# Attention's scores, maxima, p @ v and output projection ordered by an account of the PSUM buffers

## The chip, the cores and the metric

The kernel runs on one core of one Trainium2 chip. The metric is the device time of one execution in microseconds. The kernel before took 1170.13 us (median of three runs, 1167.9 to 1170.29). One more execution was recorded by the hardware profiler; the rows below are from it.

Engines are named as in the profile: PE is TensorE's matrix multiplication and PEld its weight load, DVE is VectorE, ACT is ScalarE, POOL is GpSimd, SP is the queue that issues the DMAs.

## The reference

One transformer block in which attention and a dense layer run side by side on the same normalised input, S = 2048 rows, D = 448, 16 heads of width 28 that share one key and one value head:

```python
x = A_x
xn = _layernorm(x, axis=-1)
q = (xn @ wq).reshape(B, S, H, Dh).transpose(0, 2, 1, 3)
k, v = xn @ wk, xn @ wv
scores = jnp.einsum("bhqd,bkd->bhqk", q, k) * (Dh ** -0.5)
p = softmax(scores, axis=-1)
o = jnp.einsum("bhqk,bkd->bhqd", p, v)
attn = o.transpose(0, 2, 1, 3).reshape(B, S, H * Dh) @ wo
mlp = relu(xn @ w1) @ w2
return x + attn + mlp
```

## The kernel before, in words

The program has three stretches. First the input is normalised and multiplied by the three projections; q, k and v go to DRAM in two parts each (a rounded value and its remainder), from where they are loaded again as stacks that contract over 112 rows. Then comes the dense layer, 28 tasks of two steps (`mlp_up`, `mlp_down`). Last comes attention. The change touches only attention, which starts when the last task of the dense layer has been issued.

**Units and blocks.** Attention has 16 units (`NU`): four blocks of 512 queries by four groups of four heads. A unit has 16 key blocks (`NKB`) of 128 keys. For one key block of one unit PE makes four scores (L557, one per head, 128 keys by 512 queries, in a PSUM tile `a`, after the maxima are done also in `m`), ACT takes the exponential of each (L559, into an SBUF tile `p`), and `pv` (L425) multiplies the four `p` by the values: 4 calls of L429 that add into 32 of the 128 partitions each of the PSUM tile `o`. The profile shows each call as two matmuls, so 8 per block.

**Maxima.** The softmax subtracts each query's maximum over the keys. It is found ahead of the scores: a second product (L306, queries by 512 keys, PSUM tile `m`) that DVE reduces (L310). A unit needs 64 of these products, all units 1024. 192 of them run during the dense layer's last tasks, 832 in attention; when a unit has all of its maxima, `max_all` (L318 to L320) joins them on DVE and `max_rows` (L323) turns them on PE, copies them on ACT (L329) and writes them by DMA into the two extra rows of the unit's query stack, which is why a unit's scores can start only after that.

**Buffers.** PSUM has 3 tiles `a`, 4 tiles `m` and 1 tile `o`. An `m` comes free when DVE has read it, an `a` when ACT has; a matmul into a tile that has not come free waits on PE, and all of PE's later work behind it, since PE takes its instructions in order. There are 24 tiles `p`, enough for six blocks.

**The order.** The order is written out per key block, called a step. `FIRST_OF` = "SMSMSMSMVX" and `OTHERS` = "MSMSMSMSX" say what PE gets: S is a score with its exponential, M a maximum, V the `pv` of the four blocks of the group before (`PVB` = 4), X the side work due at this step. `n_max` leaves out some M so that the 832 are spread evenly over the blocks up to eight before the last unit. So each V has four blocks, and comes once every four blocks, behind the first four scores of the next group.

**What follows a unit.** When a unit's last block has been through `pv`, ACT copies `o` out (L434), `dens` sends the sums of the exponentials to a tile `d` by four small DMAs (L457), and side work is put down: `recips` four steps on (DVE's reciprocal L463, then a DMA to DRAM and four back into `rb`), `normalized` seven steps on (POOL, L472 to L476), and after the last unit of a query block four `o_proj` (L479, 12 matmuls each into an `m`, added to `acc` by DVE at L491 and written out), one per step from nine steps on. For the last query block the first three groups of heads are projected by `o_proj_part` (L496) in 12 pieces of three matmuls, and `finish` (L509) does the last unit. `load_stack(u + 4)` (L287) issues the four DMAs of a later unit's query stack at the start of unit `u`.

## Time and profile before

| | us |
|---|---|
| runs: median (lowest to highest) | 1170.13 (1167.9 to 1170.29) |
| the profiled execution | 1169.32 |
| its span, first to last instruction | 1167.5 |
| granted clock of PE, mean | 0.999 |
| start of attention (first L557) in the span | 395.9 |
| last maximum's product ends, about | 1093.8 |
| last `pv` starts | 1154.6 |

The profiled execution's time is 1.8 us longer than its span. A row of a timeline is: start and length in us, engine, line, operation, tiles written and read, shapes, how many instructions were joined in the row, and in square brackets the idle time of the engine just before it with what ended it. A row of the waits is: engine, tile and line, what it waited for, total us, times, longest us. A row of the windows is: stretch, its length, then for each engine its busy us and the number of its instructions. In a busy group: line, engine, operation, tiles, shapes, count, busy us, mean ns of one, idle us before them.

### The profile page before, as it was taken

To read this page: it belongs to the slowest core of one execution; us is meant where nothing else is said; L and a number is where in the kernel's file an instruction comes from. 1 tells how busy PE (TensorE), PEld (TensorE's weight loads), DVE (VectorE), ACT (ScalarE), POOL (GpSimd) and SP (SyncE) were. 2 spreads that over 40 slices of the span, in tenths; PEclk is the share of its full clock that TensorE was granted. 3 is DMA by queue.
4 is the path that set the end of the run, shared out by engine and by line. 5 is a ranking of instruction groups with operands and counts; after the bars stand their busy time and mean duration, and the time that the engine had idled before them with its cause. 6 is when DMAs were issued, how large, how long until landed. Compare 5 with 4: busy or idle time off the path is not lost.

```text
span 1167.5 us, 15326 instructions
## 1 busy us (share of the span) xinstructions
PE 1151.4 (99%) x5908; PEld 731.5 (63%) x5908; DVE 791.2 (68%) x1393; ACT 583.6 (50%) x1166; POOL 115.5 (10%) x96
## 2 busy tenths in 40 slices
PE   8999999999999999999999999999999999999998
PEld 7888888778888754545456555556555545655435
DVE  6733338887788777777776878786687778586402
ACT  4311110001100467667665767675576767476784
POOL 2323022020200201010010101101011011010110
PEclk9999999999999999999999999999999999999999
DMA  8581610001000101101102010111101100000000
GB/s 254 207 177 43 145 34 1 1 1 35 1 1 1 29 1 42 32 11 43 28 16 64 11 42 16 28 33 34 43 8 42 33 11 11 32 12 1 11 10 32
DMA packets 34431, 45.94 MB, mean 39 GB/s; under 512 B 10056, under 2 KB 21000, under 8 KB 34192
## 3 DMA queue, kind: packets, MB, share of 16 engines
q1 hardware_dynamic: 34360, 44.98, 14.5%
q8 instruction: 46, 0.75, 0.3%
q14 instruction: 25, 0.20, 0.1%
HBM read 32.37 MB, written 12.18 MB: 38 GB/s over the span
## 4 chain that ended last, share of the span: by engine, by line
PE 83%; DVE 12%; ACT 3%; issue 1%; SPq 0%; DMA 0%; POOL 0%; ACTq 0%; DVEq 0%
PE a L557 21%; PE o L429 19%; PE m L306 18%; PE a L161 12%; DVE nmx L310 8%; PE a L164 3%; PE m L486 3%; PE a L360 3%; PE o L360 3%; DVE acc L365 2%; ACT p L559 2%; DVE hL L348 1%; ACT hH L347 1%; PE m L504 1%; PE m L557 1%
## 5 line engine op out<-in xcount | busy, mean ns | idle before, releaser
L310 DVE TENSOR_REDUCE nmx<-m 128x1 f32<-128x512 f32 x1024 | 625.9, 680 | 147.6 <-PE m L306 147.3
L559 ACT ACTIVATE p<-a 128x512 f32<-128x512 f32 x975 | 494.2, 658 | 181.1 <-PE a L557 180.5
L306 PE MATMUL m<-kst,qst 112*128 112x512 f32 x1024 | 401.8, 408 | 3.4 <-DVE nmx L310 1.8
L557 PE MATMUL a<-qst,kst 114*128 114x512 f32 x975 | 397.1, 419 | 5.0 <-ACT p L559 4.6
L557 PEld LDWEIGHTS a<-qst,kst 114*128 114x128 f32 x975 | 183.3, 188 | 141.1 <-ACT p L559 122.5
L306 PEld LDWEIGHTS m<-kst,qst 112*128 112x128 f32 x1024 | 194.2, 190 | 83.9 <-issue 42.8
L429 PE MATMUL o<-p,vtile 128*32 128x512 f32 x2048 | 233.0, 595 | 0.0
L347 ACT ACTIVATE hH<-a 128x512 fp32r<-128x512 f32 x56 | 33.5, 599 | 274.1 <-PE a L164 274.1
L429 PEld LDWEIGHTS o<-p,vtile 128*32 128x32 f32 x2048 | 60.0, 109 | 138.1 <-issue 132.6
L161 PE MATMUL a<-xH,w 128*128 128x512 f32 x432 | 135.1, 394 | 1.9 <-POOL w L126 1.9
L348 DVE SCALAR_TENSOR_TENSOR hL<-a,hH 128x512 fp32r<-128x512 f32 x56 | 38.7, 692 | 91.3 <-ACT hH L347 91.2
L161 PEld LDWEIGHTS a<-xH,w 128*128 128x128 f32 x432 | 81.4, 189 | 18.5 <-POOL w L126 2.2
L472 POOL TENSOR_TENSOR on<-rb,oS 128x512 f32<-128x512 f32 x15 | 19.4, 1293 | 671.2 <-DMA rb<-rscr 298.9
L161 PE MATMUL a<-xL,w 128*128 128x512 f32 x216 | 84.9, 393 | 0.0
L360 PE MATMUL a<-w,hH 128*128 128x448 f32 x224 | 63.8, 366 | 0.0
L360 PE MATMUL o<-w,hH 128*128 128x448 f32 x224 | 63.7, 366 | 0.0
L161 PEld LDWEIGHTS a<-xL,w 128*128 128x128 f32 x216 | 40.8, 189 | 8.9 <-DVE xL L212 0.3
L360 PEld LDWEIGHTS a<-w,hH 128*128 128x128 f32 x224 | 42.0, 188 | 5.8
L360 PEld LDWEIGHTS o<-w,hH 128*128 128x128 f32 x224 | 42.2, 188 | 4.6
L164 PE MATMUL a<-xR,w 128*128 128x512 f32 x144 | 44.9, 393 | 0.1
L365 DVE TENSOR_TENSOR acc<-o,acc 128x448 f32<-128x448 f32 x56 | 34.6, 618 | 14.1 <-PE o L360 14.1
L360 PE MATMUL o<-w,hL 128*128 128x448 f32 x112 | 40.9, 365 | 0.0
(94 smaller groups left out, 572.3 us busy)
## 6 DMA issues: line engine op xcount, KB each, us to landing
qst<-qscr SPq DMA_DIRECT2D x64, 224.0 KB
qscr<-qs SPq DMA_DIRECT2D x16, 512.0 KB
rb<-rscr SPq DMA_DIRECT2D x60, 64.0 KB
acc<-in_A_x SPq DMA_DIRECT2D x16, 224.0 KB
out<-acc SPq DMA_DIRECT2D x16, 224.0 KB
stg<-in_B_w SPq DMA_DIRECT2D x7, 448.0 KB
stg<-in_B_w SPq DMA_DIRECT2D x7, 384.0 KB
d<-oS SPq DMA_DIRECT2D x60, 2.0 KB
```

The lines of the kernel that those rows point to most:

```text
L161: nc.tensor.matmul(ps, lhs[:, wi, c, cols], xm[:, c, xs], start=n == 0, stop=False)
L164: nc.tensor.matmul(ps, lhs[:, wi, DC, cols], xR[:, xs], start=False, stop=wi == 1)
L306: nc.tensor.matmul(pm, qst[u][0:KQ, j, s * P : (s + 1) * P], kst[0:KQ, k0 : k0 + QB], start=True, stop=True)
L310: nc.vector.tensor_reduce(nmx[u][:, n, h : h + 1], pm, axis=AX.X, op=ALU.max)
L347: nc.scalar.activation(hH[:, f], ph, AF.Relu)
L348: nc.vector.scalar_tensor_tensor(hL[:, f], ph, 0.0, hH[:, f].bitcast(F32), op0=ALU.max, op1=ALU.subtract)
L360: nc.tensor.matmul(py[:, 0:D], hm[:, f, i * P : (i + 1) * P], wd[:, wi, f, :], start=n == 0, stop=n == 3 * FC - 1)
L365: nc.vector.tensor_tensor(acc[:, t, :], py[:, 0:D], acc[:, t, :], op=ALU.add)
L429: nc.tensor.matmul(o_acc[u][32 * j : 32 * j + 32], vtile[:, kb, :], p, start=kb == 0, stop=kb == NKB - 1)
L486: nc.tensor.matmul(py[:, 0:D], om[:, i * P : (i + 1) * P], wm[:, g, :], start=n == 0, stop=n == 3 * NHG - 1)
L557: nc.tensor.matmul(pt, kst[0 : KQ + 2, kb * P : (kb + 1) * P], st, start=True, stop=True)
L559: nc.scalar.activation(p, pt, AF.Exp, scale=SCALE)
```

## The change

The order per step is replaced by a loop that keeps an account in nanoseconds: `t` is PE's time, `act` and `dve` the starts of the two readers' latest work, `rings` the times at which the buffers `a` and `m` come free, `blocks` the key blocks whose scores are issued, with the time at which their exponentials are done. The account runs when the program is built; the program on the chip is again a fixed order. In each round of the loop one thing is issued:

- a score or a maximum while a buffer for it is free by the account (of the two, the one whose reader has less to do; maxima keep to the same even spread, up to `SLACK` = 6 ahead or behind);
- else, if an `o_proj` is waiting in `fill` and an `m` is free within 100 ns, and fewer than `MIN_V` = 3 blocks are ready or no maxima are left, that `o_proj`;
- else `pv` of all blocks of this unit that are ready, if they are three or more (two, if no buffer comes free within 100 ns); a unit's last blocks are taken together;
- else it waits for whichever buffer comes first.

So the number of blocks per V is no longer fixed. The side work of a unit is counted from the block being scored when its last `pv` is issued: `recips` 3, `normalized` 6 and the projections 8 blocks later, where before it was 4, 7 and 9 from the next unit's start. `o_proj` goes to `fill` and is issued by the rule above; `o_proj_part` is now 4 pieces of nine matmuls. `load_stack(u + 4)` is issued after the first block of unit `u` instead of ahead of it. Buffers, tiles, arithmetic and the number of instructions of each kind stay as they were. After the last maximum a score takes an `m` when that ring's next buffer is free earlier than that of `a` by the account and nothing is in `fill`, where before it alternated.

```diff
-    ppool = ctx.enter_context(tc.tile_pool(name="ppool", bufs=(PVB + 2) * HG, reuse_waits="tile"))
+    P_BUFS = 24
+    ppool = ctx.enter_context(tc.tile_pool(name="ppool", bufs=P_BUFS, reuse_waits="tile"))
...
-    FIRST_OF, OTHERS = "SMSMSMSMVX", "MSMSMSMSX"
-    side = {}
+    side, fill = {}, []
...
-            step = (u + 1) * NKB
             dens(u)
-            at(step + 4, recips, u)
-            at(step + 7, normalized, u)
+            at(step + 3, recips, u)
+            at(step + 6, normalized, u)
             if units[u][1] == NHG - 1:
-                for i in range(TPB):
-                    at(step + 9 + i, o_proj, u, i)
+                at(step + 8, fill.extend, [(o_proj, (u, i)) for i in range(TPB)])
             if u == NU - 2:
...
+                at(step + 8, fill.extend, [(o_proj_part, (u, i)) for i in range(TPB)])
...
+    T_MM, T_PV, T_MODE, T_EXP, T_MAX, T_PROJ = 232, 860, 280, 478, 597, 202
+    TO_ACT, TO_DVE, ACT_OUT, DVE_OUT = 430, 450, 745, 730
+    left, SLACK, MIN_V, WAIT = len(mx_todo), 6, 3, 100
+    spread_over = HG * ((NU - 1) * NKB - 8)
...
+    def ready():
+        n = 0
+        while n < len(blocks) and blocks[n][3] <= t and blocks[n][0] == blocks[0][0]:
+            n += 1
+        return n if n and (blocks[0][1] or t >= acc_free) else 0
...
+    while n_s < n_all or blocks:
+        step = n_s // HG
+        room = n_s < n_all and n_open < P_BUFS
+        n_max = left - len(mx_todo)
+        due = min(left, n_s * left // spread_over)
+        wants = mx_todo and n_max < due + SLACK and mx_todo[0][0] in qst
+        rest = rings["M"][0] - t
+        pool = "M" if not mx_todo and not fill and rings["M"][0] < rings["A"][0] else "A"
+        wait_s = max(0, rings[pool][0] - t) if room and (n_max + SLACK >= due or not wants) else None
+        wait_m = max(0, rest) if wants else None
+        n_v = ready()
+        tail = NKB - blocks[0][1] if blocks else 0
+        if n_v < tail <= MIN_V + 1 and room:
+            n_v = 0
+        least = min((w for w in (wait_s, wait_m) if w is not None), default=None)
+        if least == 0:
+            if wait_s == 0 and wait_m == 0:
+                what = "S" if act <= dve else "M"
+            else:
+                what = "S" if wait_s == 0 else "M"
+        elif fill and rest <= WAIT and (not mx_todo or n_v < MIN_V):
+            what = "F"
+        elif n_v >= MIN_V or n_v >= 2 and (least is None or least > WAIT) or n_v and (n_s == n_all or not room):
+            what = "V"
...
+        if what == "S":
+            t = max(t, rings[pool][0])
...
+            u, kb, p = score(pool)
...
+            act = max(act + T_EXP, t + TO_ACT)
+            rings[pool] = rings[pool][1:] + [act + ACT_OUT]
+            t += T_MM
...
+                if kb == 0 and u:
+                    load_stack(u + 4)
...
+        elif what == "V":
+            for u, kb, pp, _ in blocks[:n_v]:
+                pv(step, u, kb, pp)
+                t += T_PV
...
```

**Where the order moves.** PE in the middle of attention, before: the end of a group of four blocks and the `pv` of the group ahead of it. `a` is a score's tile, `m` a maximum's, `o` the accumulator of `pv`, `qst` and `kst` the query and key stacks.

```order
L557 MATMUL a<-qst,kst 128x512 x3
L306 MATMUL m<-kst,qst 128x512
L557 MATMUL a<-qst,kst 128x512
L306 MATMUL m<-kst,qst 128x512
L557 MATMUL a<-qst,kst 128x512
L306 MATMUL m<-kst,qst 128x512
L557 MATMUL a<-qst,kst 128x512
L306 MATMUL m<-kst,qst 128x512
L429 MATMUL o<-p,vtile 32x512 x16
L306 MATMUL m<-kst,qst 128x512
```

The same engine and stage after the change, where 11 scores and 10 maxima alternate between two `pv`.

```order
L544 MATMUL a<-qst,kst 128x512
L307 MATMUL m<-kst,qst 128x512
L544 MATMUL a<-qst,kst 128x512
L427 MATMUL o<-p,vtile 32x512 x12
L307 MATMUL m<-kst,qst 128x512
L544 MATMUL a<-qst,kst 128x512
```

A `pv` of four blocks (16 calls) after 29 to 31 scores and maxima has become one of two, three or four blocks, mostly after about 21, and the places where scores stood without a maximum between them are nearly gone. Over all of attention 64 batches of four blocks have become 92: 33 of two blocks, 47 of three, 11 of four and one of five. 81 of them come before the last maximum is far behind and hold 229 blocks; the last 11 hold 27.

PE near the end, where no maxima are left, before:

```order
L557 MATMUL a<-qst,kst 128x512
L557 MATMUL m<-qst,kst 128x512
L429 MATMUL o<-p,vtile 32x512 x16
L557 MATMUL a<-qst,kst 128x512
L557 MATMUL m<-qst,kst 128x512
```

And after the change:

```order
L544 MATMUL a<-qst,kst 128x512
L427 MATMUL o<-p,vtile 32x512 x8
L544 MATMUL m<-qst,kst 128x512 x2
L544 MATMUL a<-qst,kst 128x512
L544 MATMUL m<-qst,kst 128x512
```

Before, 16 scores stand between two `pv` of four blocks here; now 8 stand between two of two blocks.

More of the change, by code (lines that the diff above doesn't have):

```diff
@@ L492, in o_proj, with o_proj_part @@
         nc.sync.dma_start(out[t * P : (t + 1) * P, :], acc[:, t, :])
-    o_parts = {}
-    def o_proj_part(u, i, g):
+    def o_proj_part(u, i):
         b, last_g = units[u]
-        if g == 0:
-            o_parts[i] = psM.tile([P, QB], F32, name="m")
-        oH, oL = o_hl[b * NHG + g]
-        py, c = o_parts[i][:, 0:D], slice(i * P, (i + 1) * P)
-        for n, (om, wm) in enumerate(((oH, woH), (oH, woL), (oL, woH))):
-            nc.tensor.matmul(py, om[:, c], wm[:, g, :], start=g == 0 and n == 0, stop=g == last_g and n == 2)
-        if g == last_g:
-            t = b * TPB + i
-            nc.vector.tensor_tensor(acc[:, t, :], py, acc[:, t, :], op=ALU.add)
+        pt = psM.tile([P, QB], F32, name="m")
+        py, c = pt[:, 0:D], slice(i * P, (i + 1) * P)
+        for g in range(last_g + 1):
+            oH, oL = o_hl[b * NHG + g]
+            for n, (om, wm) in enumerate(((oH, woH), (oH, woL), (oL, woH))):
+                nc.tensor.matmul(py, om[:, c], wm[:, g, :], start=g == 0 and n == 0, stop=g == last_g and n == 2)
+        t = b * TPB + i
+        nc.vector.tensor_tensor(acc[:, t, :], py, acc[:, t, :], op=ALU.add)
     def finish(u):
@@ L535, in finish @@
             nc.sync.dma_start(out[t * P : (t + 1) * P, :], acc[:, t, :])
-    left = len(mx_todo)
-    spread_over = (NU - 1) * NKB - 8
-    group, ready = [], []
-    for u in range(NU):
-        if u:
-            load_stack(u + 4)
-        for kb in range(NKB):
-            step = u * NKB + kb
-            n_max = max(0, min(left, (step + 1) * left // spread_over) - (left - len(mx_todo)))
-            order = FIRST_OF if kb % PVB == 0 else OTHERS
-            skip = order.count("M") - n_max if kb % PVB == 0 else 0
-            ps = []
-            for what in order:
-                if what == "S":
-                    if mx_todo or len(ps) % 2 == 0:
-                        pt = psA.tile([P, QB], F32, name="a")
-                    else:
-                        pt = psM.tile([P, QB], F32, name="m")
-                    st = qst[u][0 : KQ + 2, len(ps), :]
-                    nc.tensor.matmul(pt, kst[0 : KQ + 2, kb * P : (kb + 1) * P], st, start=True, stop=True)
-                    p = ppool.tile([P, QB], F32, name="p")
-                    nc.scalar.activation(p, pt, AF.Exp, scale=SCALE)
-                    ps.append(p)
-                elif what == "M":
-                    if skip > 0 or not n_max:
-                        skip -= 1
-                        continue
-                    n_max -= 1
-                    done = max_tile()
-                    if done is not None:
-                        at(step + 1, max_rows, done, max_all(done))
-                elif what == "X":
-                    for f, a in side.pop(step, ()):
-                        f(*a)
-                elif what == "V":
-                    for done in ready:
-                        pv(*done)
-                    ready = []
-            group.append((u, kb, ps))
-            if len(group) == PVB:
-                ready, group = group, []
@@ L579, in attention_plus_mlp, with score @@
-    assert not side and not mx_todo
-    for done in ready:
-        pv(*done)
+    T_MM, T_PV, T_MODE, T_EXP, T_MAX, T_PROJ = 232, 860, 280, 478, 597, 202
+    TO_ACT, TO_DVE, ACT_OUT, DVE_OUT = 430, 450, 745, 730
+    left, SLACK, MIN_V, WAIT = len(mx_todo), 6, 3, 100
+    spread_over = HG * ((NU - 1) * NKB - 8)
+    t = act = dve = acc_free = 0
+    rings = {"A": [0] * NA, "M": [0] * NM}
+    blocks, ps, n_s, n_open = [], [], 0, 0
+    def score(pool):
+        u, kb, j = n_s // (HG * NKB), n_s // HG % NKB, n_s % HG
+        pt = psA.tile([P, QB], F32, name="a") if pool == "A" else psM.tile([P, QB], F32, name="m")
+        st = qst[u][0 : KQ + 2, j, :]
+        nc.tensor.matmul(pt, kst[0 : KQ + 2, kb * P : (kb + 1) * P], st, start=True, stop=True)
+        p = ppool.tile([P, QB], F32, name="p")
+        nc.scalar.activation(p, pt, AF.Exp, scale=SCALE)
+        return u, kb, p
@@ L585 @@
+    assert not side and not mx_todo and not fill, (side.keys(), len(mx_todo), fill)
 _INS = ["A_x", "A_wq", "A_wk", "A_wv", "A_wo", "B_w1", "B_w2"]
```

51 lines of the change are left out of this document (44 added, 7 removed).

## The prediction

> **What bounds the kernel now.** I read the page's busy times first, then the windows of attention's stages, the waits in the longest, and its timeline.
>
> ```profile
> PE 1151.4 (99%) x5908; PEld 731.5 (63%) x5908; DVE 791.2 (68%) x1393; ACT 583.6 (50%) x1166; POOL 115.5 (10%) x96
> PEclk9999999999999999999999999999999999999999
> ```
>
> ```profile
> 406.80:1095.50 688.70, 687.12 (x3708) 367.95 (x3707) 511.73 (x880) 464.42 (x938) 47.80 (x43) 1.00 0.10 25
> 1095.50:1154.60 59.10, 55.65 (x322) 27.91 (x321) 3.32 (x8) 46.96 (x96) 3.20 (x3) 1.00 0.02 6
> ```
>
> ```profile
> ACT p L559 <- PE a L557: 172.2, 54, 6.3
> DVE nmx L310 <- PE m L306: 146.3, 54, 3.1
> PEld a L557 <- ACT p L559: 108.7, 508, 0.5
> ```
>
> The clock is granted in full all along, so distances between PE's rows can be compared anywhere. The stage with maxima takes 688.7 us. PE's busy time there is 687.1, but a matmul's row is longer than the distance to the next one, so that figure says nothing of gaps. ACT is busy 67% of the stage and DVE 74%. They wait in turn: 54 times (about once per group of four blocks) ACT and DVE stand idle until PE brings new work, and 508 times a weight load for a score waits for ACT. Engines that wait for each other by turns mean that no engine is full. The Trainium skill (Perfetto Trace Analysis, Identifying the Most-Contended Engine) says that matmul busy time does not tell how near PE is to its limit; by that rule PE's 99% is no bar to a gain, and the timeline agrees:
>
> ```profile
> 694.00 3.64 PE L429 MATMUL o<-p,vtile 128*32 128x512 f32 x32
> 697.57 0.50 PE L306 MATMUL m<-kst,qst 112*128 112x512 f32 x1
> 697.91 0.39 PE L557 MATMUL a<-qst,kst 114*128 114x512 f32 x1
> 698.11 8.54 DVE L310 TENSOR_REDUCE nmx<-m 128x1 f32<-128x512 f32 x14 [2.31 <-PE m L306]
> 698.34 7.95 ACT L559 ACTIVATE p<-a 128x512 f32<-128x512 f32 x16 [3.58 <-PE a L557]
> 698.38 0.40 PE L557 MATMUL a<-qst,kst 114*128 114x512 f32 x1
> ...
> 698.85 0.64 PE L557 MATMUL a<-qst,kst 114*128 114x512 f32 x2
> 698.99 0.19 PEld L557 LDWEIGHTS a<-qst,kst 114*128 114x128 f32 x1 [0.18 <-ACT p L559]
> ...
> 700.06 0.41 PE L557 MATMUL a<-qst,kst 114*128 114x512 f32 x1
> 700.54 0.42 PE L557 MATMUL a<-qst,kst 114*128 114x512 f32 x1
> ...
> 702.50 1.40 PE L557 MATMUL a<-qst,kst 114*128 114x512 f32 x3
> 703.74 0.40 PE L306 MATMUL m<-kst,qst 112*128 112x512 f32 x1
> ...
> 705.21 0.39 PE L306 MATMUL m<-kst,qst 112*128 112x512 f32 x1
> 705.53 3.64 PE L429 MATMUL o<-p,vtile 128*32 128x512 f32 x32
> ...
> 709.10 0.50 PE L306 MATMUL m<-kst,qst 112*128 112x512 f32 x1
> ```
>
> One group lasts from 705.53 back to 694.00, 11.53 us. Unhindered, a score or maximum follows the last by 0.233 (697.91 to 698.38 holds two). A `pv` of four blocks holds PE for 3.57 (705.53 to 709.10); ACT and DVE run dry in it, 3.58 and 2.31 us. Afterwards PE is too fast for them: a pair of score and maximum takes 0.49 (702.50 is five pairs after 700.06), ACT's pace, and where three scores stand alone (702.50 to 703.74) each takes 0.41. The order puts `pv` where PE would have work anyway and lets PE wait where `pv` could have run.
>
> **PE's own work in attention.** Further rows, of the page, the chain and the timeline: groups of the two readers, an `o_proj`, one of the pieces of `o_proj_part`, attention's start and end.
>
> ```profile
> L310 DVE TENSOR_REDUCE nmx<-m 128x1 f32<-128x512 f32 x1024 | 625.9, 680 | 147.6 <-PE m L306 147.3
> ```
>
> ```profile
> 609.43 2.44 PE m L486 x12
> ```
>
> ```profile
> 395.88 0.63 PE L557 MATMUL a<-qst,kst 114*128 114x512 f32 x2
> 398.28 0.50 PE L557 MATMUL a<-qst,kst 114*128 114x512 f32 x1 [1.07 <-ACT p L559]
> ```
>
> ```profile
> 1137.84 0.37 PE L504 MATMUL m<-woH,oH 128*128 128x448 f32 x1
> 1138.05 0.37 PE L504 MATMUL m<-woL,oH 128*128 128x448 f32 x1
> ...
> 1154.62 3.64 PE L429 MATMUL o<-p,vtile 128*32 128x512 f32 x32
> ```
>
> From 395.9 to the end of the last `pv` (1154.62 + 3.57 = 1158.2) are 762.3 us. The work in it:
> - 1024 scores and 832 maxima by 0.233: 432.4.
> - 256 blocks of `pv`. The 32 matmuls of four blocks stand in eight fours, 0.43 apart, so 0.86 a block and 3.44 of the 3.57: 220.2.
> - What a batch costs beside its blocks: on entry 705.53 - 705.21 - 0.233 = 0.09, on leaving 3.57 - 3.44 = 0.13, and the first matmul behind it 697.91 - 697.57 - 0.233 = 0.11. Together 0.33; 64 batches, 21.1.
> - 12 `o_proj` by 2.45 (the row, 2.44): 29.4. The 36 matmuls of `o_proj_part` by 0.205: 7.4.
>
> Sum 710.5. So PE waits 51.8 us of the 762.3. Of these, 42 lie in the stage with maxima: its 57 groups have 912 scores and 815 maxima (402.4), 57 batches (57 x 3.77 = 214.9) and 29.4 of projection, 646.7 of 688.7.
>
> **The change, part by part.**
>
> *More batches.* 92 instead of 64: 28 x 0.33 = 9.2 us more on PE. The Trainium skill (TensorEngine Tiling, Key Properties) says that a change of tiling mode drains TensorE, and `pv` runs in 32-column tiles between full-width matmuls, which speaks against shorter batches. A drain to the modelled end of the last matmul would put the entry at 0.16 (its 0.39 less 0.233) in place of 0.09: 28 x 0.07 = 2 us more. The rows start `pv` before that end, so I keep 9.2.
>
> *Waits between two `pv`.* Now mostly 11 scores and 10 maxima in turn. Do they fit without a wait? A reader starts 0.43 after its matmul (697.91 to 698.34). DVE takes one per (8.54 - 0.68) / 13 = 0.605, ACT one per 0.488 (702.50 is five pairs after 700.06). A buffer is back 0.76 after its reader's start (698.34 to the fourth score: the load at 698.99, its matmul 0.11 later, as elsewhere). With four `m`, the tenth maximum needs the sixth read: 0.43 + 5 x 0.605 + 0.76 = 4.22, and PE comes to it at 9 x 0.466 = 4.19: 0.03 short. With three `a`, the eleventh score needs the eighth's reader: 0.43 + 7 x 0.488 + 0.76 = 4.61, and PE comes at 4.66: no wait. Then `pv` follows, 1.72 + 0.33 or 2.58 + 0.33, in which both readers finish what is left (three tiles, 1.8 us for DVE). So a segment of 21 costs about 0.04 of waiting; over 81 batches 3 us in place of 42. Bounds: nothing, and 0.25 a segment (one load's wait of 0.18 and some), 20 us.
>
> *`pv` and its exponentials.* In the 81 batches the last `p` read belongs to a score at least three scores back. The score issued last could only start once the exponential three before it was done, since there are three `a`. So `pv` waits for nothing new; nothing is queued behind such a wait.
>
> *The end, without maxima.* Rows of before:
>
> ```profile
> 1104.86 3.64 PE L429 MATMUL o<-p,vtile 128*32 128x512 f32 x32
> ...
> 1111.44 0.64 ACT L559 ACTIVATE p<-m 128x512 f32<-128x512 f32 x1
> ...
> 1111.92 0.65 ACT L559 ACTIVATE p<-a 128x512 f32<-128x512 f32 x1
> ...
> 1112.62 0.50 PE L557 MATMUL a<-qst,kst 114*128 114x512 f32 x1 [0.24 <-ACT p L559]
> ...
> 1114.27 3.64 PE L429 MATMUL o<-p,vtile 128*32 128x512 f32 x32
> ```
>
> Four blocks take 9.41. ACT's pace here is 0.48. Now eight scores and two blocks alternate: PE 8 x 0.233 + 1.72 + 0.33 = 3.9, ACT 8 x 0.48 = 3.8, and seven buffers keep ACT supplied during the 2.05 of a batch. PE is the bound by a little, 7.8 for four blocks. The gain is in the 51.8. At the very end the last `pv` (three blocks, straight behind eight scores) needs the eighth exponential: 0.54 + 7 x 0.48 + 0.76 = 4.7 after the batch before, while PE reaches that block at 0.24 + 1.86 + 1.72 = 3.8: 0.9 us of waiting that was not there before.
>
> *Start.* The 1.1 us at 398.28 (ACT's first exponentials come late) stay.
>
> *Side work.* `recips` now comes at least 13 scores after the unit's last `pv`. DVE would wait if `d` had not landed, and the maxima behind it, and so PE. Rows of a unit's end in the last stage:
>
> ```profile
> 1118.10 0.60 ACT L434 ACTIVATE oS<-o 128x512 f32<-128x512 f32 x1 [1.12 <-issue]
> 1118.72 2.44 SPq L457 DMA_DIRECT2D d<-oS  x4
> 1122.35 0.25 DVE L463 RECIPROCAL r<-d 128x16 f32<-128x16 f32 x1 [26.20 <-DMA d<-oS]
> ```
>
> `d` lands 3.6 us after its issue, which comes right behind the copy of `o`, some 0.9 us after the `pv`. Thirteen scores are a segment (4.9), a batch (2.05) and two pairs (0.9): 7.8 us. So 6.9 us lie between issue and use; 3.3 to spare, cost nothing. On SP's queue the stack load (four DMAs) now stands right before `d` in four units, with two small DMAs between in a fifth, behind `d` in six; the stack itself is wanted by maxima only a unit later. `o_proj` fills PE as before; its DVE addition waits as before. Both at nothing.
>
> *Sum.* 762.3 becomes 710.5 + 9.2 + 3.2 + 0.9 + 1.1 = 724.9, 37.4 less. The profiled execution took 1169.3 (span 1167.5 and 1.8 around it), 0.8 below the runs' median. So 1169.3 - 37.4 = 1131.9, and against the median's level 1132.7: **1133 us**.
>
> **The rivals.**
>
> *The readers still set the pace.* If ACT and DVE hold PE to 0.49 a pair, as in the rows at 700, the 830 pairs lose 0.024 each, 20 us: 1133 - 3 + 20 = **1150**. For it: the account uses 0.478, 0.597, 0.28 and 0.745 where I read 0.488, 0.605, 0.33 and 0.76, all a little short, so it may think buffers free that aren't. Against: pairs run at 0.47 when the rings are empty (697.91 to 698.85), and a segment now ends before they are full.
>
> *`d` comes late.* In five units `d` queues behind a stack load.
>
> ```profile
> qst<-qscr SPq DMA_DIRECT2D x64, 224.0 KB
> GB/s 254 207 177 43 145 34 1 1 1 35 1 1 1 29 1 42 32 11 43 28 16 64 11 42 16 28 33 34 43 8 42 33 11 11 32 12 1 11 10 32
> ```
>
> 0.9 MB at the highest rate here, 254 GB/s, are 3.5 us, so `d` would land 7.1 after its issue, 0.2 after it is wanted; at half the rate 3.5 later: 5 x 3.7 = 18 us, **1151**.
>
> *PE has nothing to give (slower).* If the 51.8 us are no waits that other work can fill but PE's own (each matmul released by a semaphore paying for the release, wherever it stands), they stay whole, and the 28 batches come on top: 1170.1 + 9.2 = **1179**. It decides as soon as less than 9.2 of the 51.8 come back. For it: PE's 99%. Against: 508 loads wait for ACT by name, and matmuls that carry the same waits run at 0.233 when the buffer is long free.
>
> *The change does nothing.* Were the gain spent on waits of 0.46 before each of the 81 batches (the 37.4 over 81), the time would stay at 1170. No row shows such a wait, two loads' waits together would make it.
>
> **How the numbers follow.** The forecast has 0.60, the readers' pace 0.25, a late `d` 0.04, no change 0.04, slower 0.07. Some 0.2% is what a measurement of this kernel can tell from no change. Faster by more than that: 0.60 + 0.25 + 0.04 = 0.89; same 0.04; slower 0.07. The predicted time is the forecast's. The range goes from no waits at all and matmuls at 0.230 (1133 - 3 - 6 = 1124) up to the readers' pace and 2 us of drains (1152); it leaves out the last two cases and half of what lies at its edges.
>
> **What would show it.** In the changed profile: between two `pv` pairs 0.466 apart, and loads waiting for ACT far below 108.7 us in this stage; ACT's idle time cut into more and shorter pieces (about 80, each near 1 to 2 us, not 3.6); the stage with maxima some 31 us shorter; a `pv` of two blocks followed by a score at 1.85 us; `pv` in the end stage about 3.9 us apart. Wrong, if pairs stay at 0.49, if a batch costs more than 0.33 beside its blocks, if `pv` rows wait for ACT, or if `r<-d` waits for its DMA while maxima queue behind it.

## The result and the profile after

| | before | after |
|---|---|---|
| median of 4 runs | 1170.2 us (1167.9 to 1170.8) | **1140.9 us** (1140.0 to 1141.2) |
| profiled execution, its span | 1169.3, 1167.5 | 1140.9, 1138.9 |
| attention: first score to end of the last `pv` | 762.3 | 734.6 |

The ratio of after to before is 0.9752, with a 95% interval of 0.9735 to 0.9768. The change gains 29.3 us; 37.4 were forecast (1133). 27.7 of the gain lie in attention; the first score also starts 0.9 us sooner (394.98 in place of 395.88), in a stage that the change doesn't touch. Over the profiles of this study, e11 left out, that start lies between 394.5 and 397.5. It goes with the granted clock of the first 50 us: six profiles have 0.97 there (before, e1, e3b, e4, e8, e10) and start attention at 395.9 or later, seven have 1.00 and start it at 395.8 or sooner. So 1 to 2 us of a single profile say nothing of the order of attention.

First the page's busy times, then the windows of the two stages of attention (with and without maxima), then the waits inside the first of them.

```profile
PE 1127.3 (99%) x5908; PEld 755.6 (66%) x5908; DVE 792.9 (70%) x1393; ACT 584.8 (51%) x1166; POOL 115.3 (10%) x96
```

```profile
406.80:1069.50 662.70, 662.49 (x3691) 389.55 (x3690) 512.04 (x878) 462.45 (x930) 44.80 (x41) 1.00 0.11 26
1069.50:1129.60 60.10, 59.49 (x357) 31.37 (x355) 4.88 (x11) 52.02 (x106) 5.10 (x5) 1.00 0.02 6
```

```profile
ACT p L546 <- PE a L544: 169.4, 78, 3.3
DVE nmx L311 <- PE m L307: 134.3, 81, 2.9
...
PEld a L544 <- ACT p L546: 14.7, 62, 0.8
```

PE's share is 99% in both kernels: as the prediction said, that figure cannot show the 28 us that went. The window shows them: the stage with maxima is 26.0 us shorter (688.7 to 662.7), the end 2.6 shorter (62.7 to 60.1). The waits show how. Loads of scores waited 508 times for ACT, 108.7 us in all; now 62 times, 14.7 us. ACT's own idle time has hardly changed (172.2 to 169.4), but it comes in 78 pieces of 2.2 us on average in place of 54 of 3.2, and the longest is 3.3 in place of 6.3. The readers idle nearly as much as before (DVE 134.3 for 146.3). It is PE that idles less. A load's wait is not yet a wait of PE, though; what PE itself loses is added up below.

The timeline of a middle piece, with starts and lengths in us. The rows that are left out go on in the same rhythm.

```profile
701.49 0.50 PE L544 MATMUL a<-qst,kst 114*128 114x512 f32 x1
701.82 0.40 PE L307 MATMUL m<-kst,qst 112*128 112x512 f32 x1
...
703.45 0.39 PE L544 MATMUL a<-qst,kst 114*128 114x512 f32 x1
703.64 0.10 PEld L328 LDWEIGHTS a<-ident,nm 128*32 128x32 f32 x1 [0.23 <-ACT p L546]
...
704.13 0.19 PEld L544 LDWEIGHTS a<-qst,kst 114*128 114x128 f32 x1 [0.26 <-ACT p L546]
704.14 0.50 PE L544 MATMUL a<-qst,kst 114*128 114x512 f32 x1
...
704.63 0.19 PEld L544 LDWEIGHTS a<-qst,kst 114*128 114x128 f32 x1 [0.19 <-ACT p L546]
...
706.94 1.92 PE L427 MATMUL o<-p,vtile 128*32 128x512 f32 x16
...
708.80 0.50 PE L544 MATMUL a<-qst,kst 114*128 114x512 f32 x1
...
709.38 0.40 PE L544 MATMUL a<-qst,kst 114*128 114x512 f32 x1
...
711.26 0.40 PE L544 MATMUL a<-qst,kst 114*128 114x512 f32 x1
...
713.14 0.39 PE L544 MATMUL a<-qst,kst 114*128 114x512 f32 x1
713.31 0.19 PEld L307 LDWEIGHTS m<-kst,qst 112*128 112x128 f32 x1 [0.20 <-DVE nmx L311]
713.37 0.44 PE L307 MATMUL m<-kst,qst 112*128 112x512 f32 x1
...
713.64 0.39 PE L544 MATMUL a<-qst,kst 114*128 114x512 f32 x1
```

From 709.38 to 711.26 are four pairs, 0.47 each: PE's own pace, where before a pair took ACT's 0.49. A `pv` of two blocks (706.94) is followed by the next score after 1.86. Near the end of the segment one load, that of the tenth maximum, waits for DVE (713.31); the score behind it comes 0.27 after the maximum (713.37 to 713.64), 0.04 late. And in the segment that begins at 701.49, `max_rows` takes a third `a` for its transposed maxima (703.64): two of the loads behind it wait for ACT again.

Rows at attention's start and in the stage without maxima, in the same columns:

```profile
396.17 0.40 PE L307 MATMUL m<-kst,qst 112*128 112x512 f32 x1
397.39 0.50 PE L544 MATMUL a<-qst,kst 114*128 114x512 f32 x1 [0.82 <-ACT p L546]
...
1071.88 0.27 PE L328 MATMUL a<-ident,nm 128*32 128x128 f32 x1 [0.61 <-ACT p L546]
...
1073.01 1.92 PE L427 MATMUL o<-p,vtile 128*32 128x512 f32 x16
...
1076.92 1.93 PE L427 MATMUL o<-p,vtile 128*32 128x512 f32 x16
...
1080.83 1.92 PE L427 MATMUL o<-p,vtile 128*32 128x512 f32 x16
...
1089.71 2.78 PE L427 MATMUL o<-p,vtile 128*32 128x512 f32 x24
...
1126.02 3.67 PE L427 MATMUL o<-p,vtile 128*32 128x512 f32 x24
```

The first wait is 397.39 - 396.17 - 0.23 = 0.99 us (1.1 forecast). Two blocks in the end stage take 3.91 (3.9 forecast). The last `pv` of three blocks takes 3.67 where another takes 2.78 (1089.71): 0.9 of waiting, as forecast.

**The account of PE.** The prediction's own bookkeeping can be made for every kernel here: from the first score to the end of the last `pv` PE has 689.4 us of work (432.4 + 220.2 + 29.4 + 7.4), each batch of `pv` costs 0.331 beside its blocks (0.093 on entry, 0.133 on leaving, 0.105 at the first matmul behind it, measured again over the 92 batches of after), and the rest is waiting. In the table all but the batches is in us, and "first score at" is counted from the span's start. In after, 734.6 - 689.4 - 92 x 0.331 = 14.8 us. The table goes with the experiments below.

| kernel | time | batches | first score at | attention | switches | waits |
|---|---|---|---|---|---|---|
| before | 1170.2 | 64 | 395.9 | 762.3 | 21.2 | 51.7 |
| after | 1140.9 | 92 | 395.0 | 734.6 | 30.5 | 14.8 |
| e1_even4 | 1161.1 | 64 | 396.1 | 754.1 | 21.2 | 43.5 |
| e2b_even2 | 1155.4 | 128 | 395.1 | 748.9 | 42.4 | 17.1 |
| e3b_even34 | 1160.2 | 80 | 396.4 | 752.2 | 26.5 | 36.3 |
| e8_strict34 | 1159.3 | 80 | 397.0 | 752.5 | 26.5 | 36.6 |
| e9_strict332 | 1152.8 | 96 | 395.8 | 745.7 | 31.8 | 24.5 |
| e10_ten | 1148.2 | 103 | 397.5 | 740.3 | 34.1 | 16.8 |
| e4_minv4 | 1151.7 | 64 | 396.0 | 744.5 | 21.2 | 33.9 |
| e5_minv2 | 1145.5 | 106 | 395.4 | 739.0 | 35.1 | 14.5 |
| e6_account | 1142.6 | 95 | 395.6 | 735.9 | 31.4 | 15.1 |
| e7_unfilled | 1145.2 | 97 | 395.5 | 738.1 | 32.1 | 16.6 |
| e12_rows | 1141.7 | 92 | 394.5 | 733.9 | 30.5 | 14.0 |
| e11_rings43 | 1173.3 | 110 | 409.5 | 753.7 | 36.4 | 27.9 |

### The profile page after: what moved, and what is told of

It reads as the page before. It is cut to its first block, busy times and chain, and to the rows that moved or that the text cites. A ratio compares the mean times of both kernels' runs of the same rounds, so it can differ in the third digit from the quotient of the medians.

```text
span 1138.9 us, 15294 instructions
## 1 busy us (share of the span) xinstructions
PE 1127.3 (99%) x5908; PEld 755.6 (66%) x5908; DVE 792.9 (70%) x1393; ACT 584.8 (51%) x1166; POOL 115.3 (10%) x96
## 4 chain that ended last, share of the span: by engine, by line
PE 85%; DVE 11%; ACT 2%; DMA 1%; issue 0%; POOL 0%; SPq 0%; ACTq 0%; DVEq 0%
PE a L544 21%; PE o L427 20%; PE m L307 18%; PE a L162 12%; DVE nmx L311 7%; PE a L165 3%; PE m L480 3%; PE a L361 3%; PE o L361 3%; DVE acc L366 2%; PE m L544 1%; DVE hL L349 1%; ACT hH L348 1%; ACT p L546 1%; PE m L496 1%
## 5 line engine op out<-in xcount | busy, mean ns | idle before, releaser
L307 PE MATMUL m<-kst,qst 112*128 112x512 f32 x1024 | 396.4, 405 | 2.2 <-DVE nmx L311 0.6
L544 PE MATMUL a<-qst,kst 114*128 114x512 f32 x972 | 390.0, 408 | 1.0 <-ACT p L546 0.8
L307 PEld LDWEIGHTS m<-kst,qst 112*128 112x128 f32 x1024 | 194.4, 190 | 69.2 <-DVE nmx L311 28.5
L427 PE MATMUL o<-p,vtile 128*32 128x512 f32 x2048 | 239.7, 597 | 0.0
L427 PEld LDWEIGHTS o<-p,vtile 128*32 128x32 f32 x2048 | 57.6, 109 | 130.2 <-issue 123.9
```

The costliest lines, as they stand in the source:

```text
L307: nc.tensor.matmul(pm, qst[u][0:KQ, j, s * P : (s + 1) * P], kst[0:KQ, k0 : k0 + QB], start=True, stop=True)
L427: nc.tensor.matmul(o_acc[u][32 * j : 32 * j + 32], vtile[:, kb, :], p, start=kb == 0, stop=kb == NKB - 1)
L544: nc.tensor.matmul(pt, kst[0 : KQ + 2, kb * P : (kb + 1) * P], st, start=True, stop=True)
```

## The experiments

Three theories of where the gain comes from. **A, the rings:** PE waits when the scores and maxima between two `pv` are more than three `a` and four `m` can take, so the time is the work, 0.33 a batch, and waits that the length of a segment sets; any order with such segments would do. **B, evenness:** what matters is that scores and maxima alternate evenly, whatever the length. **C, the account:** it has to know at each step which reader is behind; a fixed rule of the same length won't get there. Below, a segment is what stands between two `pv`, written (scores, maxima); it is plain if it has neither `max_rows` nor a projection. Its wait is the sum of the distances between its matmuls beyond 0.234 each, and beyond the switch at its first matmul. Six kernels start from the kernel before and change its fixed order, six start from the changed kernel.

### Fixed orders: e1, e2b, e3b

**e1_even4** keeps batches of four blocks and only spreads the maxima evenly by the count of scores:

```
-    FIRST_OF, OTHERS = "SMSMSMSMVX", "MSMSMSMSX"
+    FIRST_OF, OTHERS = "SMSMSMSMVX", "SMSMSMSMX"
...
-                    if skip > 0 or not n_max:
-                        skip -= 1
+                    due = min(left, (step * HG + len(ps)) * left // (spread_over * HG))
+                    if left - len(mx_todo) >= due:
                         continue
```

> The kernel before with one thing altered: a maximum is issued behind a score whenever the even spread, counted in scores instead of in blocks, has one due, so no three scores stand together; p @ v stays at four blocks every four blocks, 64 batches. Theory A, the rings: with three tiles a the sixteenth score of a group cannot be issued before 0.54 + 12 x 0.488 + 0.76 = 7.16 us after the first, however evenly the maxima stand, so a group falls from 11.53 to about 11.1 or 11.2; 57 x 0.36 = 20 us less than 1170, so 1150 (1145 to 1157). Theory B, evenness: the bare scores were the loss, and evenness alone gives all that the change gave or more, 1125 to 1142. Theory C, the account: only placing p @ v by the readers' state helps, so 1165 to 1171.

Measured 1161.1 us (1159.6 to 1161.7), ratio 0.9927 (0.9911 to 0.9942). No theory named this. Evenness alone is worth 9 us, 8 of them waits. Its timeline, just after a `pv`:

```profile
695.81 0.64 PE L555 MATMUL a<-qst,kst 114*128 114x512 f32 x2
...
696.29 0.40 PE L306 MATMUL m<-kst,qst 112*128 112x512 f32 x1
696.44 0.19 PEld L555 LDWEIGHTS a<-qst,kst 114*128 114x128 f32 x1 [0.19 <-ACT p L557]
...
699.23 0.40 PE L306 MATMUL m<-kst,qst 112*128 112x512 f32 x1
```

832 maxima spread evenly over 928 scores leave out about every tenth place, so that two scores stand side by side there. At 695.81 that fills the three `a` early, and from then on each score waits for ACT: from 696.29 to 699.23 are six pairs of 0.49. So (16,14) still costs 0.56 us where before it cost 0.75. Theory A had left out the neighbours.

**e2b_even2** is e1 with batches of two blocks (the pool of `p` keeps its 24 tiles):

```
-    PVB = 4
-    ppool = ctx.enter_context(tc.tile_pool(name="ppool", bufs=(PVB + 2) * HG, reuse_waits="tile"))
+    PVB = 2
+    ppool = ctx.enter_context(tc.tile_pool(name="ppool", bufs=6 * HG, reuse_waits="tile"))
```

> As the evenly spread order, but p @ v of two blocks every two blocks, fixed, without any account: 128 batches. Theory A, the rings: segments of 15 scores and maxima never fill a ring, so PE does its 689 us of work in attention, 128 x 0.33 = 42 us of switches and some 4 us of waits, 735 in all against 734.6 in the changed kernel: 1141 (1138 to 1147). Theory B, evenness: the switches only add, so above the evenly spread order with four blocks by 64 x 0.33 = 21 us. Theory C, the account: less than half of the change's gain, 1156 to 1171.

Measured 1155.4 us (1154.9 to 1156.5), ratio 0.9882 (0.9867 to 0.9897). No theory named this: A had the direction, but only some 4 us of waits, and its time is missed by 14; the measured one lies just below C's range. The waits fell to 17.1 us, but 128 batches pay 42.4 us of switches, 21.2 more than before. Short segments do away with most of the waits; their price is the switch. Its timeline shows what is left:

```profile
706.57 0.71 PE L555 MATMUL a<-qst,kst 114*128 114x512 f32 x2
706.78 0.19 PEld L555 LDWEIGHTS a<-qst,kst 114*128 114x128 f32 x1 [0.26 <-ACT p L557]
707.12 0.40 PE L306 MATMUL m<-kst,qst 112*128 112x512 f32 x1
707.27 0.19 PEld L555 LDWEIGHTS a<-qst,kst 114*128 114x128 f32 x1 [0.19 <-ACT p L557]
```

Here, too, the waits begin at two scores in a row. The 68 plain segments of (8,7) with such neighbours wait 0.12 us each, 11 without them 0.05 and those of (8,8), also without, 0.02.

**e3b_even34** is e1 with batches of three blocks and one of four in a unit:

```
-    PVB = 4
+    PVB, OPENS, CLOSES = 4, (0, 3, 6, 9, 12), (2, 5, 8, 11, 15)
...
-            if len(group) == PVB:
+            if kb in CLOSES:
```

> As the evenly spread order, with fixed batches of 3, 3, 3, 3 and 4 blocks in each unit: 80 batches, 12 fewer than the changed kernel has. Theory A, the rings: 689 of work, 80 x 0.33 = 26.5 of switches; a segment of 12 scores waits about 0.2 us for its last score, one of 16 about 0.4, together 16 us, and 2 us at the ends: 734, so 1141 (1136 to 1147), the same as with two blocks and as with the account. Theory B, evenness: near the evenly spread order with four blocks, 5 us above it. Theory C, the account: 1156 to 1171.

Measured 1160.2 us (1159.2 to 1162.1), ratio 0.9923 (0.9906 to 0.9940): no better than e1, inside C's range and 19 us above A's number. Waits fell by 7.2, switches rose by 5.3. (12,10) still waits 0.42 and (12,11) 0.25, all with neighbouring scores.

### Strict alternation: e8, e9, e10

**e8_strict34** is e3b without neighbours inside a segment: a `pv` stands between two scores, everything else alternates, and maxima run up to six ahead of their share so that hardly any is skipped in between (twelve plain segments still lack one).

```
-    FIRST_OF, OTHERS = "SMSMSMSMVX", "SMSMSMSMX"
+    FIRST_OF, OTHERS = "SMSMSMSVX", "SMSMSMSMX"
...
+                    due = (step * HG + len(ps)) * left // (spread_over * HG)
+                    if not mx_todo or left - len(mx_todo) >= due + AHEAD:
                         continue
```

> The same fixed batches as e3b_even34 (3, 3, 3, 3 and 4 blocks in each unit, 80 of them, no account); only the place of the missing maxima differs: a segment begins and ends with a score and alternates strictly between (12 scores, 11 maxima), maxima may run up to six ahead of the spread. Theory A, the rings, in the form that the first four runs leave: two scores side by side inside a segment fill the three tiles a early and every later pair then goes at ACT's pace, so what counts is strict alternation and the segment's length; waits of 0.2 us for 12 scores and 11 maxima (as the changed kernel has), 0.35 to 0.55 where two scores stand together or 16 are in a row: 21 us, with the ends 30, and 26.5 of switches: 689.4 + 56.5 = 746 in attention, 1154 (1150 to 1157), 6 us under e3b_even34. Theory C, the account: it is the placing by the readers' state, so a fixed order stays where e3b_even34 was, 1158 to 1163.

Measured 1159.3 us (1158.6 to 1160.7), ratio 0.9912 (0.9893 to 0.9930): the number of C, 5 us above A's. Waits in the whole run, then rows of the timeline:

```profile
PEld m L306 <- DVE nmx L310: 60.9, 212, 1.1
...
PEld a L555 <- ACT p L557: 25.3, 92, 1.3
```

```profile
697.10 0.19 PEld L306 LDWEIGHTS m<-kst,qst 112*128 112x128 f32 x1 [0.20 <-DVE nmx L310]
...
697.69 0.50 PE L306 MATMUL m<-kst,qst 112*128 112x512 f32 x1
...
698.29 0.50 PE L306 MATMUL m<-kst,qst 112*128 112x512 f32 x1
```

Strict alternation does what it was meant to: loads that wait for ACT fall to 92. But with a maximum for every score DVE is the slower reader, and four `m` carry it for about ten. From there on a pair takes 0.60, DVE's pace (697.69 to 698.29). A segment of (12,11) waits 0.24, one of (16,15) 0.72; the long batch of each unit makes one of (16,15) or (16,14). With neighbouring scores the same shapes waited 0.25 (e3b) and 0.38 to 0.39 (e3b, e1). So from twelve scores on strict alternation gains nothing: it changes only which reader is late.

**e9_strict332** cuts the same order into batches of 3, 3, 2, 3, 3 and 2 blocks, so that no segment has 16 scores:

```
-    PVB, OPENS, CLOSES, AHEAD = 4, (0, 3, 6, 9, 12), (2, 5, 8, 11, 15), 6
+    PVB, OPENS, CLOSES, AHEAD = 4, (0, 3, 6, 8, 11, 14), (2, 5, 7, 10, 13, 15), 6
```

> Strict alternation as in e8_strict34, with fixed batches of 3, 3, 2, 3, 3 and 2 blocks in each unit: 96 batches, near the 92 of the changed kernel, without any account. Theory A, the rings: 96 x 0.331 = 31.8 of switches, waits of 0.2 us in 52 segments of 12 scores, none in 28 of 8, with the rest and the ends 19: 740 in attention, 1148 (1144 to 1152). Theory C, the account: 1158 or more, as the other fixed orders.

Measured 1152.8 us (1152.3 to 1153.7), ratio 0.9859 (0.9843 to 0.9875): just above A's range, 5 us below C. Waits fell from 36.6 to 24.5 for 5.3 us of switches. (12,11) waits 0.22 and (8,7) 0.025. The length of a segment moves the waits here with no account; but whole blocks give only 8 or 12 scores, one shorter than needed and one longer.

**e10_ten** takes the `pv` out of the grid of blocks: after every tenth score come the blocks that are at least three scores back.

```
+                    n_s += 1
+                    if len(ps) == HG:
+                        blocks.append((u, kb, ps, n_s))
+                    if n_s % EACH == 0:
+                        while blocks and n_s - blocks[0][3] >= BACK:
+                            pv(*blocks.pop(0)[:3])
+                            if blocks and blocks[0][1] == 0:
+                                break
```

> No account: scores and maxima alternate strictly (maxima up to six ahead of their spread), and after every tenth score, wherever that falls in a block, p @ v takes the blocks whose last score is at least three scores back: 103 batches. The side work stays at the fixed steps of the kernel before. Theory A, the rings: what the account finds is only the length of a segment; 103 x 0.331 = 34.1 of switches, about 80 segments of 10 scores and 9 maxima that wait 0.03 each (2.4), with the turned maxima, the start and the end 10: 689.4 + 44 = 733.5 in attention, 1141 (1138 to 1145), the changed kernel's time. Theory C, the account: fixed orders have come to 1153 at best, and this one stays at 1148 or above.

Measured 1148.2 us (1146.5 to 1148.8), ratio 0.9809 (0.9796 to 0.9823). By the time alone this is C's edge. By the account of PE it is A's mechanism: waits are 16.8 us against after's 14.8, and the 72 plain segments of (10,9) behind the first segment wait 0.04 each, less than the 59 plain ones of after (0.09). The spans of the two profiled executions lie 8.1 us apart: 3.6 are switches (103 batches for 92), 2.0 waits, and 2.5 lie in the stages ahead of attention (first score at 397.5), which neither kernel touches and where the granted clock differed, as said above. The one execution of e10 with a granted clock of 1.000 took 1146.5, the others, at 0.998, 1147.9 to 1148.8; so at the full clock its time lies between A's range (up to 1145) and C's 1148. Where the waits of e10 lie the timeline of the end stage shows:

```profile
1086.48 0.19 PEld L554 LDWEIGHTS a<-qst,kst 114*128 114x128 f32 x1 [0.53 <-ACT p L556]
...
1087.14 1.92 PE L429 MATMUL o<-p,vtile 128*32 128x512 f32 x16
...
1091.38 0.19 PEld L554 LDWEIGHTS a<-qst,kst 114*128 114x128 f32 x1 [0.68 <-ACT p L556]
...
1092.04 2.78 PE L429 MATMUL o<-p,vtile 128*32 128x512 f32 x24
```

A fixed turn of `a` and `m` runs out of three `a` while an `m` is free; PE waits, and then does the `pv` that could have filled the wait. In the segments of this stage e10 waits 4.2 us, e8 6.4, e9 4.6, before 7.6; the changed kernel, which asks the account which ring frees first, waits 0.1. In the stage with maxima, the first segment left out, e10 waits about 9 us and the changed kernel 11, with 92 batches there against 81.

### One setting of the account each: e4, e5, e6, e7, e12, e11

**e4_minv4** lets a `pv` come only when four blocks are ready (or when neither a score nor a maximum may be issued, or at a unit's end):

```
-    left, SLACK, MIN_V, WAIT = len(mx_todo), 6, 3, 100
+    left, SLACK, MIN_V, WAIT = len(mx_todo), 6, 4, 100
...
-        elif n_v >= MIN_V or n_v >= 2 and (least is None or least > WAIT) or n_v and (n_s == n_all or not room):
+        elif n_v >= MIN_V or n_v >= 2 and least is None or n_v and (n_s == n_all or not room):
```

> The changed kernel with its rule for p @ v set to four ready blocks (two or three only at a unit's end): 64 batches, 28 fewer, each behind about 31 scores and maxima. Theory A, the rings: 28 x 0.33 = 9 us of switches less, but each of some 57 long segments waits about 0.4 us for its last scores in place of about 0.1 per short one, so 57 x 0.4 = 23 for 10 us: 1141 - 9 + 13 = 1145 (1141 to 1152), within 6 us of the evenly spread order with four blocks. Theory B, evenness: 9 us below the changed kernel, 1132. Theory C, the account: the batch's size matters little, 1132 to 1141, far below the evenly spread fixed order.

Measured 1151.7 us (1149.8 to 1152.1), ratio 0.9844 (0.9825 to 0.9863): inside A's range, above its middle, but 9 us below e1 and not within the 6 us that A allowed, and far above B and C. With as many batches as before, the account saves 18 us of waits by order alone; the last 11 us need more batches. (16,14) waits 0.36 here, against 0.75 before.

**e5_minv2** goes the other way:

```
-    left, SLACK, MIN_V, WAIT = len(mx_todo), 6, 3, 100
+    left, SLACK, MIN_V, WAIT = len(mx_todo), 6, 2, 100
```

> The changed kernel with p @ v allowed from two ready blocks on: 106 batches in place of 92, shorter segments. Theory A, the rings: 14 x 0.331 = 4.6 us more of switches, and some 4 us less of waits (fewer segments of 11 scores and 10 maxima, which wait 0.12 each): 1141.5 (1139 to 1144). Theory C, the account: no word on the size, so the switches alone, 1145.5.

Measured 1145.5 us (1145.1 to 1147.2), ratio 0.9798 (0.9782 to 0.9815). This is the number for switches alone, and A's is missed: 14 more batches cost 4.6 us of switches, and the waits stay (14.5). There was less to save than A took: the 0.12 of its expectation, and of e6's, is a mean that holds the first segment of attention with its 1.2 us; the 27 others of (11,10) wait 0.08. In these plans more than about 92 batches bring no fewer waits.

**e6_account** gives the account the durations that the trace shows, and tells it of the `a` that `max_rows` takes:

```
-    T_MM, T_PV, T_MODE, T_EXP, T_MAX, T_PROJ = 232, 860, 280, 478, 597, 202
-    TO_ACT, TO_DVE, ACT_OUT, DVE_OUT = 430, 450, 745, 730
+    T_MM, T_PV, T_MODE, T_EXP, T_MAX, T_PROJ = 234, 860, 330, 488, 605, 204
+    TO_ACT, TO_DVE, ACT_OUT, DVE_OUT = 430, 450, 760, 760
...
+                    if f is max_rows:
+                        act = max(act + T_EXP, t + TO_ACT)
+                        rings["A"] = rings["A"][1:] + [act + 420]
```

> The changed kernel with the account's numbers set to what the traces show (a matmul 234 ns, a switch 330, ACT 488 per tile, DVE 605, a buffer back 760 after its reader's start), and with the tile a that max_rows takes put on the account: 95 batches, segments mostly of 10 scores and 9 maxima, which wait 0.03 each, where 11 and 10 wait 0.12. Theory A, the rings: 1.0 us more of switches, 3 to 4 less of waits: 1138 (1136 to 1141). Theory C, the account: with a truer account the 13 us of waits that are left should mostly go: 1129 to 1134.

Measured 1142.6 us (1141.6 to 1143.6), ratio 0.9771 (0.9755 to 0.9787): neither. Truer figures give three more batches and the same waits (15.1): the segments with `max_rows` wait 1.8 us less in all than in after, the plain ones and the end 1.7 more. That the account's figures were a little short, as the prediction held for its rival, is not why waits remain.

**e7_unfilled** issues each `o_proj` at a fixed step, as the kernel before does, and not where the account finds nothing else:

```
-                at(step + 8, fill.extend, [(o_proj, (u, i)) for i in range(TPB)])
+                for i in range(TPB):
+                    at(step + 8 + i, o_proj, u, i)
```

> The changed kernel with the four o_proj of a query block at fixed blocks (8 to 11 after the unit's end), not held back until PE has nothing else; 97 batches in place of 92. Theory A, the rings: 5 x 0.331 = 1.7 us of switches more, and an o_proj in the middle of a segment lets the readers empty the rings just as one at its end does: 1142.5 (1140 to 1145). Rival: the filling is a main part of the gain, since 12 projections of 2.45 us cover 12 places where PE would wait: 1147 or more.

Measured 1145.2 us (1143.7 to 1146.2), ratio 0.9786 (0.9772 to 0.9799), just above A's range. About 3.4 us of the gain come from holding `o_proj` back: five batches fewer (1.7) and 1.8 of waits; another 0.5 lies ahead of attention, which this edit doesn't touch. The rival's 1147 is not reached.

**e12_rows** moves `max_rows` to stand right behind a `pv`, when the readers have emptied the rings, and tells the account of it:

```
-                at(step + 1, max_rows, done, max_all(done))
+                rows_due.append((n_s, done, max_all(done)))
         elif what == "V":
...
+            while rows_due and n_s - rows_due[0][0] >= 6:
+                act = max(act + T_EXP, t + TO_ACT)
+                rings["A"] = rings["A"][1:] + [act + 420]
+                max_rows(*rows_due.pop(0)[1:])
```

> The changed kernel with max_rows, which takes a tile a in the middle of a segment and makes the next scores wait (0.2 to 0.6 us each of 13 times by the changed kernel's trace), held back until right behind a p @ v, when the rings are empty, and its tile put on the account; 92 batches as before. Theory A, the rings: 2 to 4 us less, 1138 (1136 to 1140). Theory C, the account: same direction, no size; no change, 1141, would mean that these waits were covered by others.

Measured 1141.7 us (1139.5 to 1142.1), ratio 0.9753 (0.9740 to 0.9767): the same as after. The edit did what it says:

```profile
657.00 3.64 PE L427 MATMUL o<-p,vtile 128*32 128x512 f32 x32
660.57 0.29 PE L328 MATMUL a<-ident,nm 128*32 128x128 f32 x1
660.61 0.48 PE L307 MATMUL m<-kst,qst 112*128 112x512 f32 x1
660.93 0.39 PE L545 MATMUL a<-qst,kst 114*128 114x512 f32 x1
```

No load waits at `max_rows` any more beyond what the first load behind any `pv` waits (0.84), and the segments that hold one wait 1.0 us in all, in place of 4.9. But the plain segments, the first of attention counted in, went from 6.3 to 8.5 and those with an `o_proj` from 0.6 to 1.6: the account, at another place in its rules, made more long segments (three of (16,14) in place of one, eight of (12,11) in place of four). The cause was real and its removal paid nothing, because the order around it moved as well.

**e11_rings43** gives four buffers to `a` and three to `m`:

```
-    NA, NM = 3, 4
+    NA, NM = 4, 3
```

> The changed kernel with one PSUM tile given from the maxima to the scores (four a, three m, still seven), and the account planning with that. Theory A, the rings: with three m the maxima bind: 0.54 + 0.605 x (n - 4) + 0.76 against 0.467 x (n - 1) lets only about five pairs go without a wait; the planned order has 110 batches (36.4 us) and lets scores stand in pairs where maxima are short; waits of 0.1 to 0.2 in each segment: 689.4 + 36.4 + 18 = 744, 1152 (1146 to 1160). Rival: seven buffers are seven buffers, and the account makes up for how they are dealt out: 1139 to 1144.

Measured 1173.3 us (1172.0 to 1174.4), ratio 1.0026 (1.0015 to 1.0036): slower than all, and above A's range. Waits of the whole run, and the first score:

```profile
DVE nmx L311 <- PE m L307: 155.4, 102, 3.1
PEld m L307 <- DVE nmx L311: 145.0, 393, 1.9
```

```profile
409.51 0.40 PE L544 MATMUL a<-qst,kst 114*128 114x512 f32 x1
```

Loads of maxima wait for DVE 393 times, 145.0 us (101 times, 28.5 us in after): the slower reader has lost a buffer. In attention that costs 19.1 us over after; A had 744 us for attention, and it took 753.7. The other 14 us lie ahead of attention, whose first score comes at 409.5 in place of 395.0: the same two pools also serve the projections and the dense layer, which no expectation had counted. So this run tells that four `m` and three `a` are better for attention than three and four, and nothing of what one more buffer for both would be worth.

## Why the prediction was right in sign and kind, and 8 us too low

- **PE has time to give:** right. The stage with maxima is 26.0 us shorter (some 31 forecast), and 51.7 us of waits in attention became 14.8, although PE's busy share stayed at 99%. By the Trainium skill (Perfetto Trace Analysis, Identifying the Most-Contended Engine) that share does not tell how near PE is to its limit; this pair of traces agrees, with 99% on both sides of a gain of 29 us. The slower rival (1179) would have needed the waits to stay.
- **More batches, 9.2:** right. 28 more at 0.331 are 9.3. The entry costs 0.093, so no drain to the modelled end of the last matmul (0.16) is in these rows; e2b, e5 and e9 pay the same per batch. The Trainium skill (TensorEngine Tiling, Key Properties) says that a change of mode drains TensorE; these rows show what a change costs, 0.33 a batch, and not what that time is made of.
- **Start, end and last `pv`, `pv` and its exponentials, `d`:** right. 0.99 for 1.1; 3.91 for 3.9; 0.9 for 0.9. No `pv` waits for an exponential but the last. `d` is not late, so that rival (1151) falls too. The one row of such a wait stands where DVE has no maxima left:

```profile
1097.62 0.25 DVE L457 RECIPROCAL r<-d 128x16 f32<-128x16 f32 x1 [25.89 <-DMA d<-oS]
```

- **Waits between two `pv`, 3.2 us for 81 batches:** this is the term that failed, by size. The prediction's 5.2 us of waits (3.2 + 0.9 + 1.1) became 14.8, and attention took 734.6 us in place of 724.9. That the time is only 8 us too low, and not 9.7, is luck outside attention: its first score came 0.9 sooner, and the forecast had been raised by 0.8 because the profile of before lay that much under its median, which that of after does not. By kind, over the changed kernel's trace:

| | forecast | measured |
|---|---|---|
| 59 plain segments | 2.4 | 5.1 |
| 13 segments with `max_rows` | 0.5 | 4.9 |
| 9 with an `o_proj` alone | 0.4 | 0.6 |
| first segment, end stage, last `pv` | 2.0 | 2.2 |
| matmuls 0.2337 apart, not 0.233 | 0 | 1.2 |
| the matmuls of `max_rows` themselves | 0 | 0.5 |

The rest, 0.3, is rounding. Three things went wrong. First, the 27 plain segments of (11,10) wait 0.08 each, not 0.04. The sum that gave 0.04 (4.22 against 4.19) was right that the tenth maximum is where it becomes tight: in all 27 its load waits for DVE, as at 713.31. But the score behind it then comes 0.02 to 0.10 late, 0.055 on average, where the sum had a shortfall of 0.03. Second, the sum took every segment for one of (11,10). Ten plain ones of other shapes wait 2.1 us in all, where 0.04 each would be 0.4: four of (12,11) wait 0.20 each, one of (16,14) 0.35. Third, `max_rows` was not in the sum at all: "side work" named `recips`, the stacks and `o_proj`, but not the step that takes an `a` in the middle of a segment, 13 times in attention. It is the largest single error, 4.4 us. e12 shows that it can be removed and that the time does not follow, so 1133 was not there to be had by that edit.

- **The rival of the readers' pace (1150):** in part. The measured time lies about midway between the forecast and this rival, so it doesn't choose between them; the rows do. Pairs went back to 0.47, as the forecast had it, but the ends of longer segments run at the readers' pace, and e1, e3b and e8 show what it costs where segments stay long: 36 to 44 us of waits.
- **What makes the gain:** the mechanism of A, and not its sizes. All twelve times that A gave were too low, eleven of them by more than its range (e4 is inside); C's numbers held for e3b, e8 and e5 and, at the edge, for e10. What the waits show is that a segment must be about ten pairs. In segments of eight, two scores side by side also cost (0.12 against 0.02 to 0.05); at twelve they made no difference, since a reader is late there either way. Whole blocks of four scores, as e9 has them, miss the length; e10 meets it with a fixed rule, and its middle waits no more than the changed kernel's. B alone gives 9 us (e1). So low waits in the middle don't need the account. But no fixed order reached its time: it is ahead of e10 by 11 batches (3.6 us) and about 4 us in the stage without maxima. Whether a fixed count of eleven scores would save most of those batches too was not run, so it is not shown that they need the account.

**Open:** why 14 to 15 us of waits stay in after, e5, e6 and e12 alike, whatever of the account is changed. The rows say where they lie, and e6 and e12 that one kind can be traded for another; a version with clearly fewer waits was not found. None of the twelve kernels is measurably faster than the changed one.

## What to carry to other kernels

An engine that shows 99% can still be waiting: compare distances between its rows where it runs free with those where it doesn't, and make a sum of work, switches and waits. When two readers drain rings of few buffers, choose how many pieces of work go between two fillers from ring length and reader pace, and let the filler come at that count, not at the end of a natural block; then weigh each further cut against the cost of a switch. In such a sum list every step that takes a buffer, however small, and price each length of segment that the order really makes, not the typical one alone.

## What the runs showed of the hardware

- A change between full-width matmuls and 32-column tiles and back costs 0.33 us (0.093 in, 0.133 out, 0.105 at the first full-width matmul), the same within 0.01 us for batches of two, three or four blocks and for 64 to 128 of them (before, after, e2b, e9).
- A weight load's wait is longer than what PE loses by it: in the 27 segments of (11,10) of after the load of the tenth maximum waits 0.19 to 0.30 us for DVE, and the next score comes 0.02 to 0.10 us late.
- Two scores side by side cost more than their own wait: once the three `a` are full, each later pair runs at ACT's 0.49 (e1, from 695.81 on). Where scores and maxima alternate strictly, DVE is the late one after about ten pairs, and a pair takes 0.60 (e8, 697.69 to 698.29).
